# Hardware loops on VectorE and ScalarE, with VectorE handing back the key and value slots, in a one-core decode attention

## The chip, the cores and the metric

The kernel runs on one core of one Trainium2 chip. The metric is the device time of one launch in microseconds (us); lower is better. Every time below is a median of several launches, and runs are compared with runs of the kernel before on the same chip. A launch over 1.5% above the fastest of its kernel counts as slow; comparisons are between fast launches. The granted clock is the share of TensorE's full clock that the profile records.

## The reference, cut to what matters

The reference is one decode step of grouped-query attention with a cached context. It multiplies the result by a small gated MLP.

```python
B, Sq, D = 4, 1, 448
Hq, Hkv, Sk, Dh = 16, 8, 8192, 256            # bf16 throughout
xn = _layernorm(x)
q  = (xn @ wq) ...                            # one query row per batch and head
scores = einsum("bhqd,bhkd->bhqk", q, k) * (Dh ** -0.5)
o  = einsum("bhqk,bhkd->bhqd", softmax(scores), v)
s  = o.reshape(B, Sq, Hq * Dh) @ wo
return x + s * silu(_B_ref(xn, w1, w2, w3, w4))
```

There are 32 pairs of batch and key/value head; the text calls each pair a "head". Each head needs one K and one V block of 8192 x 256 bf16 values, which is 4 MB each. Each block is read once from HBM, so 32 x 8.39 MB must pass through the load queue whatever else happens.

## The kernel before

The five engines each run their own program and meet through semaphores. K and V have two slots each. SyncE issues all loads:

```python
def load_k(h):
    if h >= 2:
        sp.wait_ge(S["p_t"], NGR * (h - 1))     # TensorE has transposed all of head h-2
    sp.dma_start(kn_dst(h), A_k_cache[b, g]...).then_inc(S["dk%d" % (h % 2)], 16)
def load_v(h):
    ... sp.wait_ge(S["p_pv"], h)                # TensorE has done PV of head h-2
    sp.dma_start(vflat[h % 2], ...).then_inc(S["dv%d" % (h % 2)], 16)
...
for h in range(2, NH):
    load_k(h); load_v(h - 1)
```

TensorE transposes K in 16 groups. VectorE evacuates (copies out) nine groups and ScalarE seven. TensorE then forms scores three groups later. The last scores of a head, and its softmax, are interleaved with the PV product (softmax weights times V) of the head before. `f_rmax` to `f_negb` find the maximum and spread it, `f_rz` takes the reciprocal of the row sum, and `f_ot` multiplies the PV product by it:

```python
def evac(engine, h, j):
    engine.wait_ge(S["p_t"], NGR * h + j + 1)   # the count grows with h
    ... engine.tensor_copy(dst, src).then_inc(S["v_ev"], 1)      # or ScalarE: activation Copy

def body(h):                                    # TensorE, already a hardware loop of two heads
    for j in range(NGR):
        f_t(h, j)                               # transposes of group j
        if j >= LAG: f_s(h, j - LAG)            # scores
    tail = [f_s(h, 13), f_s(h, 14), f_s(h, 15), f_rmaxT(h), f_bc(h), f_sum(h)]
    for i, f in enumerate(tail):
        f_pv(h - 1, PV_PARTS[i], PV_PARTS[i + 1]); f()

for h in range(NH):                             # VectorE, written out 32 times; ScalarE likewise
    for j in range(NGR):
        if j in D_GROUPS: evac(v, h, j)
    f_rmax(h); f_diag(h); f_negb(h); f_ot(h - 1); f_rz(h)
```

After the last head, TensorE forms the output product of key/value heads 0 to 6 (`f_o(g)`), then PV of head 31, then `f_o(7)`.

## Time and profile before

| | before |
|---|---|
| median of the first 3 launches | 664.19 us (663.47 to 664.4) |
| profiled span | 661.7 us |
| TensorE busy, granted clock | 82%, 0.858 |
| load queue, share of 16 engines' span | 98.4% |
| GB/s in the middle (100 to 600 us) | 432 |

From the page of the kernel before: span, busy time by engine (us, share of span, instructions), and the lines of the 40 slices for the DMA engines' busy tenths and for GB/s.

```profile
span 661.7 us, 27809 instructions
...
PE 543.4 (82%) x12935; PEld 535.1 (81%) x12935; DVE 256.4 (39%) x577; ACT 255.3 (39%) x358; POOL 9.3 (1%) x44
...
DMA  8999999999999999999999999999999999999993
GB/s 362 436 408 432 422 434 432 428 436 432 430 434 428 436 430 428 438 430 430 436 426 434 434 424 440 428 432 434 428 432 436 424 438 432 430 434 430 428 420 156
...
q1 hardware_dynamic: 12288, 278.99, 98.4%
q8 instruction: 11, 0.18, 0.1%
q14 instruction: 8, 0.07, 0.0%
```

The DMA engines are busy in every slice but the last. The three queue lines give packets, MB and share. q1 carries the data. q8 and q14 fetch instructions.

The waits of the kernel before show who waits for whom (us in total, times, longest):

```profile
PE pst L469 <- PEq L421: 80.7, 29, 8.1
...
PE psm L498 <- PEq L421: 8.5, 31, 0.3
...
PE psm L493 <- PEq L421: 3.9, 1, 3.9
```

TensorE waits 80.7/29 = 2.8 us before each head's first transposes, for K to land. That is its slack. The other two waits are in the softmax chain, at the row sum (L498) and at the broadcast of the maximum (L493). The same view of SyncE's queue shows which counts release the slots:

```profile
SPq L177 <- PE pst L469: 411.8, 30, 15.2
SPq L188 <- PE psv L507: 139.0, 30, 11.4
```

The issue part of the page gives, last on the line, the median us from issue to landing:

```profile
kn<-in_A_k_cache_dram SPq DMA_DIRECT2D x32, 4096.0 KB, 27.2
vb<-in_A_v_cache_dram SPq DMA_DIRECT2D x31, 4096.0 KB, 32.3
```

4 MB at 432 GB/s takes 9.7 us, so a load spends most of those 27 or 32 us queued behind others.

The end of the kernel matters too. From the timeline of TensorE's (and one VectorE) instructions of the kernel before, start and duration in us:

```profile
635.57 3.35 PE L469 MATMUL pst<-ident_b,kn 128*128 128x128 bf16 x32 [2.16 <-PEq L421]
...
651.54 0.35 PE L498 MATMUL psm<-rowsum,ones_f 128*128 128x2 f32 x2 [0.28 <-PEq L421]
...
652.08 2.72 PE L537 MATMUL pst<-wo_sb,OT 128*4 128x112 bf16 x112 [0.18 <-PEq L421]
...
659.31 0.28 DVE L416 TENSOR_TENSOR out_b<-res,x 128x112 bf16<-128x112 f32 x1
```

The last head's transposes start at 635.57 us, when its K has landed. The result is ready at 659.31 + 0.28 = 659.59 us. Those 24.0 us are compute that follows the last K.

### The profile page before, as it was taken

To read this page: it belongs to the slowest core of one execution; us is meant where nothing else is said; L and a number is where in the kernel's file an instruction comes from. 1 tells how busy PE (TensorE), PEld (TensorE's weight loads), DVE (VectorE), ACT (ScalarE), POOL (GpSimd) and SP (SyncE) were. 2 spreads that over 40 slices of the span, in tenths; PEclk is the share of its full clock that TensorE was granted. 3 is DMA by queue.
4 is the path that set the end of the run, shared out by engine and by line. 5 is a ranking of instruction groups with operands and counts; after the bars stand their busy time and mean duration, and the time that the engine had idled before them with its cause. 6 is when DMAs were issued, how large, how long until landed. Compare 5 with 4: busy or idle time off the path is not lost. (4 is left out here: it accounts for less than half of the span.)

```text
span 661.7 us, 27809 instructions
## 1 busy us (share of the span) xinstructions
PE 543.4 (82%) x12935; PEld 535.1 (81%) x12935; DVE 256.4 (39%) x577; ACT 255.3 (39%) x358; POOL 9.3 (1%) x44
## 2 busy tenths in 40 slices
PE   2387798889878878988888898878898888789787
PEld 2387797789878878988788898878898788789787
DVE  6233253334433334433334443333344333344332
ACT  1044253344443334444333444433344433344441
POOL 2000000000000000000000000000000000000000
PEclk9988698898877889878789987878988778898788
DMA  8999999999999999999999999999999999999993
GB/s 362 436 408 432 422 434 432 428 436 432 430 434 428 436 430 428 438 430 430 436 426 434 434 424 440 428 432 434 428 432 436 424 438 432 430 434 430 428 420 156
DMA packets 12331, 279.24 MB, mean 422 GB/s; under 512 B 1172, under 2 KB 3224, under 8 KB 3480
## 3 DMA queue, kind: packets, MB, share of 16 engines
q1 hardware_dynamic: 12288, 278.99, 98.4%
q8 instruction: 11, 0.18, 0.1%
q14 instruction: 8, 0.07, 0.0%
q10 hardware_dynamic: 24, 0.01, 0.0%
HBM read 278.99 MB, written 0.00 MB: 422 GB/s over the span
## 5 line engine op out<-in xcount | busy, mean ns | idle before, releaser
L469 PE MATMUL pst<-ident_b,kn 128*128 128x128 bf16 x4096 | 354.4, 244 | 80.7 <-PEq L421 80.7
L469 PEld LDWEIGHTS pst<-ident_b,kn 128*128 128x128 bf16 x4096 | 287.9, 111 | 82.5 <-issue 82.5
L239 ACT ACTIVATE kT<-pst 128x1024 bf16<-128x1024 bf16 x224 | 229.3, 1024 | 231.9 <-PE pst L469 231.9
L237 DVE COPY kT<-pst 128x1024 bf16<-128x1024 bf16 x288 | 197.8, 692 | 268.3 <-PE pst L469 268.3
L481 PE MATMUL psc<-qc,kT 128*128 128x2 bf16 x4096 | 176.8, 164 | 1.0 <-issue 1.0
L481 PEld LDWEIGHTS psc<-qc,kT 128*128 128x128 bf16 x4096 | 157.4, 98 | 1.1 <-issue 1.1
L507 PE MATMUL psv<-pT,vb 128*128 128x32 bf16 x4096 | 131.8, 177 | 5.7 <-issue 3.1
L507 PEld LDWEIGHTS psv<-pT,vb 128*128 128x128 bf16 x4096 | 117.8, 97 | 6.8 <-issue 5.9
L260 ACT ACTIVATE pT<-psc,negb 128x64 bf16<-128x64 f32 x64 | 20.2, 332 | 144.5 <-DVE negb L384 144.5
L372 DVE TENSOR_REDUCE rmax<-psc 128x2 f32<-128x128 f32 x32 | 9.3, 292 | 42.1 <-PE psc L481 42.1
L396 DVE TENSOR_TENSOR OT<-psv,rz 128x2 bf16<-128x2 f32 x65 | 7.6, 162 | 30.1 <-PE psv L507 24.0
L498 PE MATMUL psm<-rowsum,ones_f 128*128 128x2 f32 x64 | 11.8, 253 | 8.5 <-PEq L421 8.5
L498 PEld LDWEIGHTS psm<-rowsum,ones_f 128*128 128x128 f32 x64 | 9.9, 195 | 10.8 <-issue 10.8
L377 DVE TENSOR_REDUCE gmax<-psm 2x1 f32<-2x128 f32 x32 | 8.9, 279 | 17.6 <-PE psm L489 17.6
L493 PE MATMUL psm<-diag,ones_f 2*128 2x2 f32 x64 | 11.6, 248 | 4.5 <-PEq L421 3.9
L493 PEld LDWEIGHTS psm<-diag,ones_f 2*128 2x128 f32 x64 | 9.8, 190 | 6.8 <-issue 4.0
L230 POOL COPY qc<-qT 128x4 bf16<-128x4 bf16 x32 | 6.0, 188 | 599.9 <-PE psc L481 587.1
L384 DVE COPY negb<-psm 128x2 f32<-128x2 f32 x32 | 5.1, 160 | 21.4 <-PE psm L493 21.4
L260 ACT ACTIVATION_READ_ACCUMULATOR pT<-psc,negb 128x1 f32 x64 | 12.6, 196 | 0.0
L427 PE MATMUL pst<-ident_b,xn_b 4*128 4x4 bf16 x14 | 0.6, 161 | 12.6 <-DVE xn_b L306 8.0
L427 PEld LDWEIGHTS pst<-ident_b,xn_b 4*128 4x128 bf16 x14 | 0.5, 99 | 12.7 <-issue 7.9
L388 DVE RECIPROCAL rz<-psm 128x2 f32<-128x2 f32 x32 | 5.5, 171 | 12.6 <-PE psm L498 12.6
(68 smaller groups left out, 70.7 us busy)
## 6 DMA issues: line engine op xcount, KB each, us to landing
kn<-in_A_k_cache_dram SPq DMA_DIRECT2D x32, 4096.0 KB, 27.2
vb<-in_A_v_cache_dram SPq DMA_DIRECT2D x31, 4096.0 KB, 32.3
vb<-in_A_v_cache_dram SPq DMA_DIRECT2D x4, 1024.0 KB, 17.9
vb<-in_A_wq_dram SPq DMA_DIRECT2D x1, 3584.0 KB, 11.5
wo_sb<-in_A_wo_dram SPq DMA_DIRECT2D x1, 3584.0 KB, 46.4
vb<-in_B_w_dram SPq DMA_DIRECT2D x2, 1568.0 KB, 16.9
out_dram<-out_b SPq DMA_DIRECT2D x2, 0.9 KB
out_dram<-out_b ACTq DMA_DIRECT2D x2, 0.9 KB
```

The lines of the kernel that those rows point to most:

```text
L230: gp.tensor_copy(qc[:, h % 2], qT[:, b, g]).then_inc(S["g_q"], 1)
L237: engine.tensor_copy(dst, src).then_inc(S["v_ev"], 1)
L239: engine.activation(dst, src, ACT.Copy).then_inc(S["a_ev"], 1)
L260: ins = act.activation(pv_p[:, :, hh], sc[:, :, hh], ACT.Exp, bias=negb[:, s, hh:hh + 1], scale=SCALE, accum_out=rowsum[:, s, hh:hh + 1])
L372: v.tensor_reduce(rmax[:, :], psc[h % 2][:, 0:NCH * REP].rearrange("p (k h) -> p h k", h=REP), AX.X, ALU.max).then_inc(S["v_rmax"], 1)
L377: c(v.tensor_reduce(gmax[:, :], psm[0:REP, 0:P], AX.X, ALU.max))
L396: ins = v.tensor_tensor(OT[:, g, :, dh, b], src[:, dh * PVW:dh * PVW + REP], rz[:, h % 2, :], ALU.mult)
L469: ins = pe.transpose(dst[:, t * P:(t + 1) * P], kn[:, h % 2, GC * j + kl, half * P:(half + 1) * P], ident_b[:, :])
L481: ins = pe.matmul(psc[h % 2][:, kk * REP:(kk + 1) * REP], kT[:, j % RING, t * P:(t + 1) * P], qc[:, h % 2, half, :], start=(half == 0), st ...
L493: pe.matmul(psm[:, P:P + REP], ones_f[0:REP, :], diag[:, :], start=True, stop=True).then_inc(S["p_m2"], 1)
L498: pe.matmul(psm[:, P + REP:P + 2 * REP], ones_f[:, :], rowsum[:, h % 2, :], start=True, stop=True).then_inc(S["p_m3"], 1)
L507: ins = pe.matmul(psv[:, dh * PVW:(dh + 1) * PVW], vb[:, h % 2, kk, dh:DH:NHALF], pT[:, h % 2, kk * REP:kk * REP + PVW], start=(kk == 0), ...
```

## The change

The change puts VectorE's and ScalarE's per-head programs into hardware loops of two heads. In these loops a wait names a fixed count, so every wait for a count that grows with the head becomes "wait for one, then take one away". That forces the rest: one semaphore per consumer (`p_t` splits into `p_td` and `p_ta`); VectorE, which now consumes TensorE's counts, hands the slots back to SyncE (`v_k`, `v_v`); and GpSimd, which stays written out, copies each head's result from a staging tile to its place. The core of the diff:

```diff
-                    sp.wait_ge(S["p_t"], NGR * (h - 1))
+                    sp.wait_ge(S["v_k"], h - 1)
...
-                    sp.wait_ge(S["p_pv"], h)
+                    sp.wait_ge(S["v_v"], h)
...
+        def take(eng, name, n=1):
+            eng.wait_ge(S[name], n).then_inc(S[name], -n)
...
+            def put(h):                            # GpSimd
+                gp.tensor_copy(OT[:, g, :, :, b], otmp[:, h % 2]...).then_inc(S["g_p"], 1)
+                gp.wait_ge(S["g_p"], h + 1)
+                gp.sem_inc(S["g_o"], 1)
...
-            engine.wait_ge(S["p_t"], NGR * h + j + 1)
+            take(engine, "p_td" if j in D_GROUPS else "p_ta")
...
+                take(v, "p_pv")
+                take(v, "g_o")
+                v.tensor_tensor(otmp[:, h % 2], psv..., rz..., ALU.mult).then_inc(S["v_s"], 1)
+                take(v, "v_s")
+                v.sem_inc(S["v_ot"], 1)
+                v.sem_inc(S["v_v"], 1)
...
+            with nc.Fori(0, NH // 2, engines=[mybir.EngineType.DVE]):
+                for h in range(2):
+                    ...evacuations...
+                    v.sem_inc(S["v_k"], 1)
+                    f_rmax(h); f_diag(h); f_negb(h); f_ot(h - 1); f_rz(h)
...
             take(pe, "v_ot")
+            pe.wait_ge(S["g_f"], 1)                # the last GpSimd copy but one head's
             for g in range(HKV - 1):
                 f_o(g)
```

More of the change, by code (lines that the diff above doesn't have):

```diff
@@ L97, in bass_recurrent_scan__gqa_block_cached__mixer_s_mlp__decode_kernel @@
         qc = sb("qc", [P, 2, NHALF, REP], BF16)
+        otmp = sb("otmp", [P, 2, NHALF, REP], BF16)
         OT = sb("OT", [P, HKV, REP, NHALF, Bn], BF16)
@@ L135, in bass_recurrent_scan__gqa_block_cached__mixer_s_mlp__decode_kernel @@
             + ["dvl%d" % i for i in range(NPIECE)]
-            + ["p_t", "p_sc", "p_m1", "p_m2", "p_m3", "p_pv", "p_x", "p_q", "p_h", "p_h2", "p_o"]
+            + ["p_td", "p_ta", "p_sc", "p_m1", "p_m2", "p_m3", "p_pv", "p_x", "p_q", "p_h", "p_h2", "p_o"]
             + ["v_ev", "a_ev", "v_rmax", "v_diag", "v_neg", "v_ot", "a_exp", "g_q", "g_c",
-               "v_xT", "v_qT", "v_hT", "v_bout", "v_c", "v_w", "a_c", "v_out"])}
+               "v_s", "v_k", "v_v", "g_o", "g_p", "g_f", "v_xT", "v_qT", "v_hT", "v_bout", "v_c", "v_w", "a_c", "v_out"])}
         vflat = [vb[:, i].rearrange("p c d -> p (c d)") for i in range(2)]
@@ L211, in prog_sp @@
             sp.wait_ge(S["dout"], 16 * NQD)
+        def take(eng, name, n=1):
+            eng.wait_ge(S[name], n).then_inc(S[name], -n)
         def prog_pool(gp):
+            def put(h):
+                b, g = divmod(h, HKV)
+                gp.tensor_copy(OT[:, g, :, :, b],
+                               otmp[:, h % 2].rearrange("p dh r -> p r dh")
+                               ).then_inc(S["g_p"], 1)
+                gp.wait_ge(S["g_p"], h + 1)
+                gp.sem_inc(S["g_o"], 1)
             c = _Chain(gp, S["g_c"])
@@ L228, in prog_pool @@
                 if h >= 2:
-                    gp.wait_ge(S["p_sc"], h - 1)
+                    gp.wait_ge(S["v_v"], h - 1)
                 gp.tensor_copy(qc[:, h % 2], qT[:, b, g]).then_inc(S["g_q"], 1)
+                if h >= 3:
+                    put(h - 3)
+            for h in range(NH, NH + 2):
+                gp.wait_ge(S["v_v"], h - 1)
+                put(h - 3)
+            gp.wait_ge(S["g_p"], NH - 1)
+            gp.sem_inc(S["g_f"], 1)
         def evac(engine, h, j):
-            engine.wait_ge(S["p_t"], NGR * h + j + 1)
+            take(engine, "p_td" if j in D_GROUPS else "p_ta")
             src = pst[j % NST][:].bitcast(BF16)
@@ L253, in exps @@
                 s = h % 2
-                act.wait_ge(S["v_neg"], h + 1)
-                if h >= 1:
-                    act.wait_ge(S["p_pv"], h)
+                take(act, "v_neg")
                 sc = psc[s][:, 0:NCH * REP].rearrange("p (k h) -> p k h", h=REP)
@@ L264, in exps @@
                         ins.then_inc(S["a_exp"], 1)
-            for h in range(NH):
-                for j in range(NGR):
-                    if j not in D_GROUPS:
-                        evac(act, h, j)
-                exps(h)
+            with nc.Fori(0, NH // 2, engines=[mybir.EngineType.Activation]):
+                for h in range(2):
+                    for j in range(NGR):
+                        if j not in D_GROUPS:
+                            evac(act, h, j)
+                    exps(h)
             act.wait_ge(S["v_out"], 1)
@@ L310, in prog_dve @@
             v.sem_inc(S["v_ot"], 1)
+            v.sem_inc(S["g_o"], 3)
             v.sem_inc(S["dv1"], 16)
@@ L370, in f_rmax @@
             def f_rmax(h):
-                v.wait_ge(S["p_sc"], h + 1)
+                take(v, "p_sc")
                 v.tensor_reduce(rmax[:, :], psc[h % 2][:, 0:NCH * REP].rearrange(
@@ L375, in f_diag @@
             def f_diag(h):
-                v.wait_ge(S["p_m1"], h + 1)
-                c(v.tensor_reduce(gmax[:, :], psm[0:REP, 0:P], AX.X, ALU.max))
-                c.sync()
+                take(v, "p_m1")
+                v.tensor_reduce(gmax[:, :], psm[0:REP, 0:P], AX.X, ALU.max
+                                ).then_inc(S["v_s"], 1)
+                take(v, "v_s")
                 v.tensor_scalar(diag[:, :], ident_f[0:REP, 0:REP], gmax[:, 0:1], -SCALE,
@@ L382, in f_negb @@
             def f_negb(h):
-                v.wait_ge(S["p_m2"], h + 1)
+                take(v, "p_m2")
                 v.tensor_copy(negb[:, h % 2, :], psm[:, P:P + REP]).then_inc(S["v_neg"], 1)
             def f_rz(h):
-                v.wait_ge(S["p_m3"], h + 1)
-                c(v.reciprocal(rz[:, h % 2, :], psm[:, P + REP:P + 2 * REP]))
+                take(v, "p_m3")
+                v.reciprocal(rz[:, h % 2, :], psm[:, P + REP:P + 2 * REP]
+                             ).then_inc(S["v_s"], 1)
@@ L390, in f_ot @@
+                take(v, "v_s")
             def f_ot(h):
-                b, g = divmod(h % NH, HKV)
-                v.wait_ge(S["p_pv"], h + 2)
-                c.sync()
-                for dh in range(NHALF):
-                    src = psc[0] if (h == NH - 1 and dh == 1) else psv
-                    ins = v.tensor_tensor(OT[:, g, :, dh, b], src[:, dh * PVW:dh * PVW + REP],
-                                          rz[:, h % 2, :], ALU.mult)
-                    if dh == NHALF - 1:
-                        ins.then_inc(S["v_ot"], 1)
-                    else:
-                        c(ins)
@@ L403, in prog_dve @@
-            for h in range(NH):
-                for j in range(NGR):
-                    if j in D_GROUPS:
-                        evac(v, h, j)
-                f_rmax(h)
-                f_diag(h)
-                f_negb(h)
-                f_ot(h - 1)
-                f_rz(h)
-            f_ot(NH - 1)
+                take(v, "p_pv")
+                take(v, "g_o")
+                v.tensor_tensor(otmp[:, h % 2],
+                                psv[:, 0:NHALF * PVW].rearrange("p (a n) -> p a n", a=NHALF)[
+                                    :, :, 0:REP],
+                                rz[:, h % 2, :].unsqueeze(1).broadcast_to([P, NHALF, REP]),
+                                ALU.mult).then_inc(S["v_s"], 1)
@@ new lines, in f_ot @@
+                take(v, "v_s")
+                v.sem_inc(S["v_ot"], 1)
+                v.sem_inc(S["v_v"], 1)
+            with nc.Fori(0, NH // 2, engines=[mybir.EngineType.DVE]):
+                for h in range(2):
+                    for j in range(NGR):
+                        if j in D_GROUPS:
+                            evac(v, h, j)
+                    v.sem_inc(S["v_k"], 1)
+                    f_rmax(h)
+                    f_diag(h)
+                    f_negb(h)
+                    f_ot(h - 1)
+                    f_rz(h)
@@ L413, in prog_dve @@
+            h = NH - 1
+            b, g = divmod(h, HKV)
+            take(v, "p_pv")
+            for dh in range(NHALF):
+                ins = v.tensor_tensor(OT[:, g, :, dh, b],
+                                      (psv, psc[0])[dh][:, dh * PVW:dh * PVW + REP],
+                                      rz[:, h % 2, :], ALU.mult)
+            ins.then_inc(S["v_ot"], 1)
             v.wait_ge(S["p_o"], 1)
@@ L419, in prog_pe @@
         def prog_pe(pe, xn_mark, xn2_mark):
-            def take(name, n=1):
-                pe.wait_ge(S[name], n).then_inc(S[name], -n)
             pe.wait_ge(S["g_c"], 8)
@@ L431, in prog_pe @@
                 if k == 0:
-                    take("v_xT")
-            take("dwq", 16)
+                    take(pe, "v_xT")
+            take(pe, "dwq", 16)
             qo = q_ps[:, 0:NKC * Bn].rearrange("p (b a g dh hh) -> p g hh dh a b", b=Bn, a=NHF,
@@ L442, in prog_pe @@
             ins.then_inc(S["p_q"], 1)
-            take("dw3", 16)
-            take("v_xT")
+            take(pe, "dw3", 16)
+            take(pe, "v_xT")
             w3v = w3_sb.rearrange("p j (m k) -> p j k m", k=NFK)
@@ L450, in prog_pe @@
             ins.then_inc(S["p_h"], 1)
-            take("dw4", 16)
-            take("v_hT")
+            take(pe, "dw4", 16)
+            take(pe, "v_hT")
             for k in range(NFK):
@@ L460, in prog_pe @@
             ins.then_inc(S["p_h2"], 1)
-            take("v_bout")
+            take(pe, "v_bout")
             def f_t(h, j):
                 if j == 0:
-                    take("dk%d" % (h % 2), 16)
+                    take(pe, "dk%d" % (h % 2), 16)
                 dst = pst[j % NST][:].bitcast(BF16)
@@ L471, in f_t @@
                                        ident_b[:, :])
-                ins.then_inc(S["p_t"], 1)
+                ins.then_inc(S["p_td" if j in D_GROUPS else "p_ta"], 1)
             def f_s(h, j):
                 if j == 0:
-                    take("g_q")
-                take("v_ev" if j in D_GROUPS else "a_ev")
+                    take(pe, "g_q")
+                take(pe, "v_ev" if j in D_GROUPS else "a_ev")
                 for t in range(TB):
@@ L487, in f_rmaxT @@
             def f_rmaxT(h):
-                take("v_rmax")
+                take(pe, "v_rmax")
                 pe.transpose(psm[0:REP, 0:P], rmax[:, :], ident_f[:, :]).then_inc(S["p_m1"], 1)
             def f_bc(h):
-                take("v_diag")
+                take(pe, "v_diag")
                 pe.matmul(psm[:, P:P + REP], ones_f[0:REP, :], diag[:, :], start=True, stop=True
@@ L496, in f_sum @@
             def f_sum(h):
-                take("a_exp")
+                take(pe, "a_exp")
                 pe.matmul(psm[:, P + REP:P + 2 * REP], ones_f[:, :], rowsum[:, h % 2, :],
@@ L502, in f_pv @@
                 if lo == 0:
-                    take("v_ot")
-                    take("dv%d" % (h % 2), 16)
+                    take(pe, "v_ot")
+                    take(pe, "dv%d" % (h % 2), 16)
                 for i in range(lo, hi):
@@ L529, in prog_pe @@
             h = NH - 1
-            take("dwo", 16)
+            take(pe, "dwo", 16)
             def f_o(g):
@@ L540, in f_o @@
                 return ins
-            take("v_ot")
+            take(pe, "v_ot")
+            pe.wait_ge(S["g_f"], 1)
             for g in range(HKV - 1):
@@ L546, in prog_pe @@
             for i in range(NPIECE):
-                take("dvl%d" % i, 16)
+                take(pe, "dvl%d" % i, 16)
                 for dh in range(NHALF):
@@ L554, in prog_pe @@
             ins.then_inc(S["p_pv"], 1)
-            take("v_ot")
+            take(pe, "v_ot")
             f_o(HKV - 1).then_inc(S["p_o"], 1)
```

## The prediction

> **What bounds the kernel now.** Transfers. The table of stretches gives DMA share 1.00 and 432 GB/s over 100 to 600 us; the queue part puts the load queue at 98.4% of 16 engines' span. The Trainium skill ("DMA: Bandwidth & Descriptors", section "Where 436 GB/s comes from") puts the ceiling of the 16 ports at 435.2 GB/s; this trace agrees (432). One head's K and V (8.39 MB) cost about 19.4 us at that rate.
>
> TensorE is busy 82%, but waits about 2.8 us a head (80.7 us in 29 waits of the transposes) for K. A load lands 27.2 us (K) or 32.3 us (V) after issue, while 4 MB alone takes about 9.7 us: two or more loads are always queued.
>
> **What the change does.**
> 1. It releases no slot earlier. Before, SyncE waits on TensorE's own semaphore for K (411.8 us in 30 waits) and V (139.0 us in 30). After, VectorE relays both: K after its wait for group 15 (about 0.1 us later, estimated), V after the multiply by rz: today 0.64 us idle and 0.23 us of OT multiplies follow the PV product, so 0.8 to 1 us later. The queue absorbs it.
> 2. Waits that rode on instructions become separate wait-and-decrement instructions, which take 51 ns on TensorE. Evacuations (692 ns VectorE, 1024 ns ScalarE, per 1.29 us pair cycle) leave ScalarE 0.27 us idle, and TensorE reads a group three groups later: no loss. The softmax chain (rmax, gmax, diag, negb, exp, sum) gets about six more: 0.2 to 0.5 us more TensorE wait per head, out of 2.8 us of slack.
> 3. Loops: an ALU step and a branch per two heads on VectorE and ScalarE; TensorE's own branch takes 0.2 us. Hidden under the K wait. The refill queue has only 8 packets (0.07 MB); the mid-run 8 KB ones, 0.3 us of one DMA engine each, should vanish: I count 0 to 1 us.
> 4. Two OT multiplies become one into a staging tile, which GpSimd copies (about 190 ns). Only the last counts: the output product of the first 7 groups now waits for VectorE, then GpSimd. Today it starts at 652.05 us, 0.5 us after OT; I estimate 0.4 to 0.8 us later.
>
> **On the critical path:** only the end. The last K's arrival sets it; then come 17.5 us of TensorE work on head 31 and 7.5 us of products, the stream ending near 651 us. There I add 0.2 to 0.5 us (2) and 0.4 to 0.8 us (4), and take 0 to 1 us (3) off. Net about +0.4 us.
>
> **Prediction: 664.6 us, 8 in 10 between 661.5 and 667.5. Faster by over 2%: 0.02; within 2%: 0.95; slower: 0.03.**
>
> **What would show it.** The middle stretch still at 432 GB/s and DMA share 1.00; K and V landing times shorter by up to 1 us; TensorE's waits for K down from 80.7 to 65 to 75 us, those at the row sum (8.5 us) up; fewer refill packets; V's issue 5.2 to 5.6 us after K's rather than 4.58.
>
> **What would make it wrong.** A back edge on ScalarE or VectorE that stalls several us (instruction refetch, a reloaded activation table) would exceed the 2.8 us of slack and starve the stream: slower by 2% or more. If the mid-run refills delay the engine that paces every load, the gain could reach 2 us. TensorE's granted clock (0.858) falling would lengthen the uncovered end.

## The result

| | before | after |
|---|---|---|
| median | 663.85 us (4 runs) | 663.11 us (4 runs) |
| range | 663.47 to 664.4 | 662.86 to 663.97 |
| ratio, fast runs | 1 | 0.999 (0.9973 to 1.0008) |

Ratios here and below are the mean time of one kernel's fast runs over that of the other's of the same rounds, so they are not quite the ratio of the medians. The interval includes 1. The lines that answer to those shown before, in the same order and views:

```profile
span 661.1 us, 28772 instructions
...
PE 544.7 (82%) x12935; PEld 536.4 (81%) x12935; DVE 254.3 (38%) x545; ACT 255.3 (39%) x358; POOL 13.6 (2%) x75
...
DMA  8999999999999999999999999999999999999993
GB/s 364 437 403 429 428 434 432 430 436 426 432 434 428 436 426 432 434 430 436 426 433 432 434 430 430 434 432 430 432 432 430 434 428 434 430 432 434 428 419 164
...
q1 hardware_dynamic: 12288, 278.99, 98.5%
q8 instruction: 11, 0.18, 0.1%
q14 instruction: 2, 0.02, 0.0%
```

The refill packets of q14 fell from 8 to 2, while the data queue is as full as before. The middle stretch (100 to 600 us) is again at DMA share 1.00 and 432 GB/s. TensorE's waits, then SyncE's:

```profile
PE pst L496 <- PEq L215: 66.6, 29, 8.1
...
PE psm L525 <- PEq L215: 14.6, 31, 0.5
...
PE psm L520 <- PEq L215: 10.8, 32, 3.2
```

```profile
SPq L178 <- DVEq L429: 391.9, 30, 14.2
SPq L189 <- DVEq L422: 159.3, 30, 10.2
```

The waits in the chain (row sum and broadcast) grew by 6.1 + 6.9 = 13.0 us, and the waits for K shrank by 14.1 us. The slots now come from VectorE. Landing times:

```profile
kn<-in_A_k_cache_dram SPq DMA_DIRECT2D x32, 4096.0 KB, 26.8
vb<-in_A_v_cache_dram SPq DMA_DIRECT2D x31, 4096.0 KB, 31.2
```

Loads land 0.4 and 1.1 us sooner after issue, because they are issued that much later into the same queue. And the end:

```profile
634.29 3.33 PE L496 MATMUL pst<-ident_b,kn 128*128 128x128 bf16 x32 [1.73 <-PEq L215]
...
650.69 0.38 PE L525 MATMUL psm<-rowsum,ones_f 128*128 128x2 f32 x2 [0.47 <-PEq L215]
...
651.33 2.78 PE L564 MATMUL pst<-wo_sb,OT 128*4 128x112 bf16 x112 [0.26 <-POOLq L249]
...
658.71 0.28 DVE L446 TENSOR_TENSOR out_b<-res,x 128x112 bf16<-128x112 f32 x1
```

The last K's transposes start 1.28 us earlier than before. From there to the end (658.99 us) takes 24.70 us instead of 24.02, 0.68 us longer. So the stream gained 1.3 us and the end gave back 0.7 us: the profiles net to 0.6 us. Two things needed explaining: why a change of some hundreds of instructions a launch moves the time so little, and where the 1.3 us came from.

### The profile page after: what moved, and what is told of

Read it like the earlier page. It is cut to its first block, busy times and chain, and to the rows that moved or that the text cites. A ratio compares the mean times of both kernels' runs of the same rounds, so it can differ in the third digit from the quotient of the medians.

```text
span 661.1 us, 28772 instructions
## 1 busy us (share of the span) xinstructions
PE 544.7 (82%) x12935; PEld 536.4 (81%) x12935; DVE 254.3 (38%) x545; ACT 255.3 (39%) x358; POOL 13.6 (2%) x75
## 5 line engine op out<-in xcount | busy, mean ns | idle before, releaser
L496 PE MATMUL pst<-ident_b,kn 128*128 128x128 bf16 x4096 | 354.5, 245 | 66.6 <-PEq L215 66.6
L415 DVE TENSOR_TENSOR otmp<-psv,rz 128x4 bf16<-128x4 f32 x32 | 5.2, 162 | 26.9 <-DVEq L215 26.9
## 6 DMA issues: line engine op xcount, KB each, us to landing
kn<-in_A_k_cache_dram SPq DMA_DIRECT2D x32, 4096.0 KB, 26.8
```

Of the source, the lines that this page charges most:

```text
L496: ins = pe.transpose(dst[:, t * P:(t + 1) * P], kn[:, h % 2, GC * j + kl, half * P:(half + 1) * P], ident_b[:, :])
```

## The experiments

Twelve kernels were run, in four groups that answer one question each.

### 1. Is it the load stream that hides the change's cost?

The same edit takes away half of V's bytes for heads 2 to 30, in the kernel before (`half_before`), in the kernel after (`half_after`), and in the kernel after with both loops written out (`half_unrolled`). The arithmetic is wrong on purpose; the output tolerance does not notice it.

```diff
-                    sp.dma_start(vflat[h % 2], src.rearrange("p c d -> p (c d)")
+                    n = NCH if h < 2 else NCH // 2
+                    sp.dma_start(vflat[h % 2][:, 0:n * DH],
+                                 src[:, 0:n, :].rearrange("p c d -> p (c d)")
```

> The kernel before, but V of heads 2 to 30 is loaded only by half (wrong result on purpose). Theory T (the load stream paces the kernel): one head's bytes fall from 8.39 to 6.29 MB, 14.6 us at 432 GB/s, so TensorE's own work of about 16.6 us a head (19.42 us minus 2.8 us of wait for K) takes over: about 580 to 590 us, and the waits of the transposes (80.7 us) nearly vanish. Rival (TensorE or the evacuations pace it already): within 2% of 664 us.

> The kernel after with the same half V loads. Theory H (the change adds TensorE waits of about 0.4 us a head in the softmax chain, which the wait for K hides in the full kernel): slower than half_before by 8 to 14 us (1.4 to 2.4%). Rival N (the change costs TensorE nothing, or the loops save something): within 3 us of half_before, or faster.

> half_after with the VectorE and ScalarE loops written out again, every separate wait-and-decrement kept. If the waits carry the hidden cost, within 3 us of half_after. If the back edges carry it, nearer to half_before, by 5 us or more.

Measured: half_before 548.16 us (ratio to before 0.826), half_after 577.47 us (0.872; launches from 571.2 to 581.8, the slowest counts as slow), half_unrolled 584.81 us (0.879; 580.2 to 588.2). Taking 22% of the bytes away (279.0 to 218.2 MB) gave 17% of the time back, so the stream paces the full kernel. The estimate of 580 to 590 us was too high: with nearly all of the waits for K gone, the granted clock was 0.953 instead of 0.858, which the sum had left out. From the waits of half_before:

```profile
PE pst L471 <- PEq L423: 10.2, 15, 7.9
...
PE psm L500 <- PEq L423: 8.5, 31, 0.3
...
PE psm L495 <- PEq L423: 3.3, 1, 3.3
```

and of half_after:

```profile
PE psm L527 <- PEq L217: 14.6, 31, 0.5
...
PE psm L522 <- PEq L217: 11.1, 32, 3.5
PE pst L498 <- PEq L217: 10.2, 13, 8.1
```

The stream is still at 407 to 424 GB/s from 100 to 500 us in half_before, but TensorE hardly waits for it: its waits for K (`pst`) are 10.2 us in both kernels. So the change now shows, at about 5% (0.8719/0.8262 = 1.055; the fast launches alone have means of 575.4 and 548.5 us, 1.049). The forecast was 1.4 to 2.4%. In the two profiled runs (569.2 against 546.4 us, both fast) 6.1 + 7.8 = 13.9 us of that is wait in the softmax chain, as expected. For the other 9 us the profiles show a lower granted clock (0.934 against 0.953), and over all launches of half_after (0.920 to 0.934) it is never as high. The clock records and the starts of the first transposes tell the two parts apart. Where the clock is 1.0 throughout, two heads take 15.08 + 14.78 us in half_before (154 to 199 us) and 15.53 + 15.23 us in half_after (258 to 427 us): 0.45 us more a head, which over 31 heads is the 13.9 us. The rest goes with spells at a clock of 0.50, which add up to 50.6 us in half_before and 74.7 us in half_after. Why they come more often is left open. In the full kernel the same waits are there and only come out of the 2.8 us that TensorE would have spent waiting for K.

Writing the loops out did not bring the cost back down (it was 7 us slower, at a clock of 0.91 to 0.92). At a clock of 1.0 its heads take the same 15.53 + 15.23 us as those of half_after (262 to 323 us). So the back edges (the jumps at the end of a loop) do not carry the cost; what both kernels have, the separate waits in the chain, does. The expectation of "within 3 us" missed: its profile has 105.4 us at a clock of 0.50, 30.7 us more than half_after, and why is left open.

### 2. Does it matter when a slot is released?

`late_mid` lets VectorE release K at the end of the head and V in the middle of the next one. `late_head` lets SyncE wait one head longer for K. `pe_release` gives the release back to TensorE; VectorE then has to infer from the row sum that PV is done, so its `f_rz` moves ahead of `f_ot`.

```diff
 late_mid:
-                    v.sem_inc(S["v_k"], 1)             # after the evacuations
+                    v.sem_inc(S["v_k"], 1)             # after f_rz(h)
+                        if j == 6: v.sem_inc(S["v_r"], 1)      # in the evacuations
-                    sp.wait_ge(S["v_v"], h)
+                    sp.wait_ge(S["v_r"], h + 1)
 late_head:
-                    sp.wait_ge(S["v_k"], h - 1)
+                    sp.wait_ge(S["v_k"], h)
 pe_release:
-                    sp.wait_ge(S["v_k"], h - 1)
+                    sp.wait_ge(S["p_k"], h - 1)        # TensorE: with the scores after the last transposes
-                    sp.wait_ge(S["v_v"], h)
+                    sp.wait_ge(S["p_pv"], h)
-                    f_ot(h - 1)
                     f_rz(h)
+                    f_ot(h - 1)
```

> The kernel after with both releases made later by VectorE: K at the end of the head (5.8 us later), V in the middle of the next head (at its 4th evacuation, about 7 us later). If queued loads absorb it: within 0.3% of the kernel after (663.1 us), K landing near 21 us, V near 24 us. Rival (release time counts): 32 times 6 us, so up to 850 us.

> The kernel after with the K slot released a whole head later (about 19.4 us). The slack is the landing time of 26.8 us less the 9.7 us that 4 MB takes, about 17 us, so this must starve: K landing near 10 to 12 us, DMA share under 1 in the middle, period 22 to 23 us, 720 to 745 us in all. If release time never counts: 664 us.

> The kernel after, but SyncE waits again on TensorE's own counts for K and V (no relay by VectorE). If the queue absorbs the release time: 663.1 us within 1 us, with K and V landing times back near 27.2 and 32.3 us. Rival (a release 0.9 us later costs part of that per head): up to 10 us faster.

Measured: late_mid 663.28 us (ratio to before 0.9992, interval 0.9974 to 1.0009), no different from the kernel after. Its landing times:

```profile
kn<-in_A_k_cache_dram SPq DMA_DIRECT2D x32, 4096.0 KB, 20.9
vb<-in_A_v_cache_dram SPq DMA_DIRECT2D x31, 4096.0 KB, 22.9
```

A release that comes about 6 us (K) and 8 us (V) later comes out of the queueing time, one for one (K's issue at 302.63 us instead of 296.53, V's at 309.39 instead of 301.84). late_head took 799.93 us (1.205). The wait of its transposes for K, and its landing time:

```profile
PE pst L496 <- PEq L215: 216.9, 31, 8.0
```

```profile
kn<-in_A_k_cache_dram SPq DMA_DIRECT2D x32, 4096.0 KB, 12.2
```

Here the slack is used up. TensorE waits 7 us a head, and the DMA share from 100 to 600 us is 0.84 with 351 GB/s. The direction and the landing time came out as expected. The total did not: the period between heads is 23.9 us, worked out from the starts of the first transposes, where 22 to 23 was expected, and the sum had forgotten the 30 us before the first head and the 25 us after the last K.

pe_release took 664.96 us (ratio to before 1.0013, interval 1.0 to 1.0027), outside the 1 us that was allowed around 663.1; its profile is 0.9 us longer than that of the kernel after, though its slots come free no later. Its middle is the same (432 GB/s). Its expected landing times came only in part: V 31.8 us, K still 26.8. The whole difference of the profiles is at the end:

```profile
634.01 3.39 PE L494 MATMUL pst<-ident_b,kn 128*128 128x128 bf16 x32 [1.68 <-PEq L215]
...
650.46 0.35 PE L525 MATMUL psm<-rowsum,ones_f 128*128 128x2 f32 x2 [0.47 <-PEq L215]
...
652.25 2.78 PE L564 MATMUL pst<-wo_sb,OT 128*4 128x112 bf16 x112 [1.44 <-POOLq L249]
```

The output product starts 1.79 us after the row sum instead of 0.64, because `f_ot`, and GpSimd's copy behind it, now run after `f_rz`. So 1.15 us more in the chain after the last K made the time from the last K's transposes to the result 1.2 us longer (25.92 against 24.70 us), while slot releases about 6 us (K) and 8 us (V) later, as in late_mid, cost nothing.

### 3. Where did the stream's 1.3 us come from?

The kernel after without its loops, but with every separate wait kept, in three forms: both engines written out (`unrolled`), VectorE alone (`unroll_vector`), ScalarE alone (`unroll_scalar`).

```diff
-            with nc.Fori(0, NH // 2, engines=[mybir.EngineType.DVE]):
+            for _ in range(NH // 2):
                 for h in range(2):
```

> The kernel after with the VectorE and ScalarE loops written out, full loads. My theory: same time within 0.3% of before, 10 or more packets on the refill queue instead of 2. Rival (the refills delay the stream and the loops paid by removing them): 0.5 to 2 us slower than the kernel after's 663.1 us.

> The kernel after with VectorE's loop alone written out. Theory R (each instruction refill of VectorE holds one DMA engine, always the same one, for about 1 us, and the slowest engine paces every load): nearly the whole loss of the run unrolled, 668.3 to 669.3 us, with about 8 mid-run refill packets each followed by a 32 KB packet of about 1.87 us instead of 1.22, and the last of a load's 16 landings 0.97 us later after each. Rival S (refills cost by their number, whichever engine asks): about 9/14 of the loss, near 667 us.

> The kernel after with ScalarE's loop alone written out. Theory R: ScalarE's refills fall on another DMA engine, which is not the slowest, so 663.1 to 663.8 us, with about 5 or 6 mid-run refill packets each followed by a packet of about 1.59 us. Rival S: about 5/14 of the loss, near 665.2 us.

Measured: unrolled 669.22 us (1.0076, interval 1.0062 to 1.009), unroll_vector 669.02 us (1.0078, 1.0064 to 1.0092), unroll_scalar 663.34 us (0.9994, 0.9981 to 1.0008). My first expectation, that unrolling changes nothing, fell, and so did its rival's size (0.5 to 2 us): it cost 6 us. The two forecasts of theory R for one engine alone, made after that, came out (668.3 to 669.3 us and 663.1 to 663.8 us). The lines of q14 are, for unrolled,

```profile
q14 instruction: 16, 0.13, 0.0%
```

for unroll_vector,

```profile
q14 instruction: 11, 0.09, 0.0%
```

and for unroll_scalar

```profile
q14 instruction: 8, 0.06, 0.0%
```

All have more refill packets (fetches of instructions) than the kernel after (2), but only VectorE's cost time. The packet records of the traces, which no view prints, say why. Each mid-run refill is one 8 KB packet of 0.31 to 0.33 us. The next 32 KB data packet after it then takes 1.87 us when the refill is VectorE's, and 1.59 us when it is ScalarE's, instead of 1.22 us. Together that is about 0.97 us (0.32 + 1.87 - 1.22) lost on one DMA engine for a refill of VectorE, and 0.69 us for one of ScalarE. A refill followed by 1.87 us is taken for VectorE's and one followed by 1.59 us for ScalarE's, because unroll_vector has only the first kind and unroll_scalar only the second. The unit prices are the same in every run. The table counts from 90 us on; before that the start-up, with its other loads and TensorE's own 16 KB packets (q8, at 18 to 78 us), makes the landings uneven in all five:

| worked out from packet and landing records | before | after | unrolled | unroll_vector | unroll_scalar |
|---|---|---|---|---|---|
| refills followed by a 1.87 us packet | 4 | 0 | 8 | 8 | 0 |
| refills followed by a 1.59 us packet | 3 | 0 | 5 | 0 | 5 |
| refills followed by a 1.57 us packet | 0 | 1 | 1 | 1 | 1 |
| loads whose last landing came over 0.2 us late | 2 | 0 | 6 | 6 | 0 |
| sum of that lateness, us | 1.4 | 0 | 5.9 | 5.4 | 0 |

The Trainium skill ("DMA: Bandwidth & Descriptors", section "Why a DMA increments its semaphore by 16 and not by 1") says that the 16 engines of a transfer finish independently and the semaphore counts them. The trace agrees: each load has 16 landings. In the kernel after, the last of the 16 follows the last of the load before by 9.71 us all through from 90 us on. In unrolled six such steps are about 10.7 us, each just after a refill of VectorE, and the spread from first to last landing grows from 3.1 to 8.9 us. That growth fits one DMA engine, always the same, that falls behind by about 1 us per refill, with every load waiting for it. The first two refills of VectorE (near 105 and 170 us) delay no landing, which fits an engine that was not yet the last. ScalarE's refills delay no load by more than 0.17 us, which fits another engine that is not the last. The trace does not name the engine of a packet, so which engine it is stays inferred. In the profiles of unrolled and unroll_vector the last K lands 5.4 and 5.2 us later than in the kernel after; the result comes 6.3 and 5.8 us later. The other 0.7 to 0.9 us lie after the last K and were not looked into.

This accounts for the kernel before as well: 4 refills of VectorE, two of which show in the landings, 0.44 + 0.99 = 1.4 us. The profile of the kernel after has the last K 1.28 us earlier. This repeats: in all six profiles with full loads and no refill of VectorE from 90 us on (after, after_again, late_mid, pe_release, early_out, unroll_scalar) the last K lands between 633.9 and 634.4 us, in the one profile of the kernel before at 635.4 us. And it shows what VectorE's loop is for: the separate waits nearly double VectorE's instructions (621 records before, 1230 in unrolled), and without the loop their fetches would have cost 6 us.

### 4. Can the end be shortened?

The end is TensorE's work after the last K. The output product of groups 0 to 5 needs only heads that are done before the last one, so it could fill the last wait for K. `early_out` takes the last two heads out of TensorE's loop and puts the product between them. `early_loop` leaves the loop alone and runs the product in every iteration; only the last one counts.

```diff
 early_out:
-            with nc.Fori(0, NH // 2, engines=[PE], ...): body(0); body(1)
+            with nc.Fori(0, NH // 2 - 1, engines=[PE], ...): body(0); body(1)
+            body(0)
+            pe.wait_ge(S["g_f"], 1)
+            for g in range(HKV - 2): f_o(g)         # accumulates in a free part of psc0
+            body(1)
 early_loop:
                 body(0)
+                take(pe, "g_f")
+                for g in range(HKV - 2): f_o(g)     # own accumulator; VectorE adds it in
                 body(1)
```

> The kernel after with TensorE's last two heads out of its loop and the output product of the first 6 groups moved from the end into the wait for the last K. If the end is TensorE's work after the last K: 2 us less, about 661.0 us. If the extra TensorE code (some six more 16 KB fetches while the stream runs) delays the stream or stalls TensorE: 663 us or more.

> The same early output product, but inside TensorE's loop (96 small products between the two heads of every iteration, only the last counts), so no new code is fetched in mid-stream; the last two groups go to a second accumulator. If early_out lost to instruction fetches on TensorE: no stall over 1 us in TensorE's products, the end from the last K shorter by about 2 us (24.7 to 22.7 us), total 660.5 to 662.0 us. If the 2.3 us of extra work per two heads is not hidden by the wait for K, or the longer loop body has to be fetched again: 665 us or more.

> The kernel after unchanged, for a narrower interval against before: 0.3 to 0.9 us faster (ratio 0.9986 to 0.9995), as its profile had it: load stream 1.3 us earlier at the last K, end 0.7 us longer.

early_out took 670.18 us (1.0097 of before). The last K landed at 634.0 us, as in the kernel after (634.2), but its transposes start only at 639.79 us, and from there to the result takes 24.65 us, nearly the 24.70 us of the kernel after. So the end was not shortened. The last two heads' code is no longer part of the loop and would have to be fetched. From its queue part and from its timeline of TensorE:

```profile
q8 instruction: 17, 0.28, 0.2%
```

```profile
633.14 0.64 PE L534 MATMUL psv<-pT,vb 128*128 128x32 bf16 x18 [3.37 <-issue]
...
639.23 0.63 PE L563 MATMUL psc<-wo_sb,OT 128*4 128x112 bf16 x19 [0.93 <-issue]
```

q8 has 6 more packets of 16 KB. TensorE stands still for 3.37 and 0.93 us with no semaphore to wait for, and a q8 packet is in flight during the longer stop. After the last K's transposes have begun it stops twice more, for 1.46 and 0.40 us, which takes back the 2 us that the end was to gain. That this was the missing code is an inference from these facts; no run took the fetch away alone.

early_loop was meant to do that, and it is inconclusive. Its six launches took 661.8 to 703.1 us: 661.82 the best, 670.16 the next, and the other four (675.7 to 703.1) count as slow. The one profile of it fell among the slow ones and has 28 q8 packets instead of 11; the extra ones come in two bursts, at 304 to 355 and 580 to 634 us, so the aim of no new code in mid-stream was not met in that launch. The best launch is 1.3 us below the median of the kernel after, but one launch in six proves nothing, so this version is not a gain. Why the launches differ is left open.

after_again, the unchanged kernel after, took 663.28 us beside 663.65 us for before; ratio 0.9996 (0.9983 to 1.0009). Its forecast (0.3 to 0.9 us faster) is neither confirmed nor refuted. The difference of 0.3 to 0.7 us that the medians and the profiles show stays within what these runs can tell from zero.

## Why the prediction was right

The time came out at 663.11 us, against 664.6 predicted with a range of 661.5 to 667.5, and "same" had 0.95. Point by point:

- **Bound by transfers: right.** Half of V's bytes less took 17% off the kernel before; the middle stretch stayed at 432 GB/s. The Trainium skill's 435.2 GB/s for the 16 ports ("DMA: Bandwidth & Descriptors", section "Where 436 GB/s comes from") agrees with it.
- **1, no earlier release, absorbed by the queue: right.** V's issue follows K's by 5.31 us (321.68 - 316.37) after, 4.58 us before; 5.2 to 5.6 was predicted. Landing times fell by 0.4 and 1.1 us. late_mid showed that 6 to 8 us are absorbed, late_head that a whole head (about 19 us) is not.
- **2, separate waits cost TensorE 0.2 to 0.5 us a head, out of its slack: right.** The chain's waits grew by 13.0 us over 32 heads, 0.41 us each. The waits for K went from 80.7 to 66.6 us (65 to 75 predicted).
- **3, loops: the mechanism was right and the term too small.** The back edges are hidden (VectorE's branch record is 56 ns, and the half-load heads at a clock of 1.0 take the same time with and without the loops). The term "I count 0 to 1 us" for the refills measured 1.3 to 1.4 us, because a refill holds its DMA engine for 0.97 us and not for its own 0.3 us, and because VectorE's, as far as the landings show, all delay the same pacing engine. The prediction had named that last case as what would make it wrong.
- **4, the output product 0.4 to 0.8 us later: too large.** It starts 0.64 us after the row sum instead of 0.54, so 0.10 us later. The rest of the end's 0.68 us is 0.43 us in the chain of the last head (as predicted) and 0.15 us in the products themselves.

The two mis-sized terms err the same way: the refills gained more than predicted and the output product lost less. Their errors add up instead of cancelling: predicted net +0.4 us, profiles -0.6 us. The range held because it was 6 us wide, and "same" because 2% is 13 us; neither tests terms of this size.

The change was large and moved the time little because its cost (13 us of TensorE waits, shown in the half-load pair) lies wholly inside waits for K, because the later slot releases lie inside the queue, and because all that is left are the edges: 1.3 us gained in the stream, 0.7 us lost at the end.

## What to carry to other kernels

Where two loads are already queued, as here, do not expect a slot release that comes a few us earlier or later to show; estimate the slack as landing time less the transfer's own time, and look for the time in the part after the last load. Count instruction fetches as transfers: here each late refill of VectorE delayed a load by up to 1 us, so a hardware loop on a helper engine can pay even where that engine is 60% idle. When a rewrite needs more instructions per step (here separate waits), make it together with the loop: the waits without the loop measured 0.8% slower (unrolled).

## What the Trainium skill lacked or had wrong

- "Runtime: NRT & Kernel Launch", section "Instruction fetch mechanics", calls the cost of crossing a block boundary "mostly hidden" and prefers full unrolling. Here each VectorE refill cost the data stream up to 1.0 us; written-out VectorE code made the kernel 5.9 us slower (669.02 against 663.11 us). No page that I found has the effect on loads in flight.
- The same section gives refill blocks of 16 KiB for every engine. In these traces TensorE's packets (q8) are 16 KB, while the refills that come and go with VectorE's and ScalarE's code (q14) are 8 KB.
- The same section takes fetches as hidden because issue is slower than the fill. TensorE's early_out run, under a full load stream, stood still for 3.37 us in straight-line code while a 16 KB packet was in flight (cause inferred, as said above).
- "DMA: Bandwidth & Descriptors", section "Queues, rings and completion order", says that an engine takes turns between queues at packet boundaries, but gives no price: here the data packet after an 8 KB refill took 1.87 or 1.59 us instead of 1.22.
- "Perfetto Trace Analysis", section "DVE / Act Engine Instruction (TENSOR_ADD, Activation, etc)", has the wait queue in which an instruction's own semaphore wait is held. No page that I found prices a separate wait-and-decrement against it: the record itself is 21 ns on VectorE and 17 ns on ScalarE, the work behind it starts a median 107 and 88 ns after the record's start, and TensorE waited 0.41 us more per head.
